# The clamp and the shift of a weight decoder, with their constants in a PSUM column

## Chip, cores, metric

The kernel runs on one core of a Trainium2 chip. The metric is the time of one execution on the device in microseconds (us); lower is better. The engines are TensorE (PE), VectorE (DVE, `V` in the code), ScalarE (ACT, `A`), GpSimd (POOL, `G`) and SyncE (SP, `DQ`), which issues transfers.

## What is computed

```python
X = np.fft.fft(np.fft.fft(x, axis=1), axis=2).real          # x: 2 x 3008 x 256
X = X.reshape(6016, 256)
X = (1 / (1 + np.exp(-(X @ w_gate))) * (X @ w_val)) @ w_out  # layer 1, width 1536
h = X @ w_in                                                 # layer 2, width 2048
out = (h * np.cos(h)) @ w_out2
```

All weights come in as float64, read by the kernel as pairs of 32-bit words, and are turned into float32 on the chip.

## The kernel before

**Work.** The transform has three stages. Stage A (up to about 40 us) multiplies sixteen chunks of x as they arrive. Stages B and C (40 to 83 us) are sixteen blocks of matmuls in a fixed order: twelve of stage B (L399/L400), whose outputs ACT casts to D2h (L419) and DVE subtracts to D2l (L423), and four of stage C (L437), copied out by DVE (L445) or ACT (L448) into `eo`, the activations. Two more blocks of stage C lie inside the first steps of layer 1. Blocks take PSUM banks in turn (`bank()`, `nbank`).

Layer 1 has 72 steps, six token groups by twelve slices of the width. In step s PE does `ab(s, 0)` into banks 4 and 5 and `ab(s, 1)` into banks 6 and 7 (L493 to L495), then the output matmuls of step s−4 (L533, L535, L536), 24 matmuls in all. DVE does `even(s)` (two L511, from banks 4 and 5) and `tokens(s)` (two L519, from banks 6 and 7); ACT the sigmoid (L667) and the high parts (L607, L608); POOL two products (L523) and an accumulating transfer (L546) into gh. `ab(s+1, 0)` waits for `even(s)`, and `ab(s+1, 1)` for `tokens(s)`. Layer 2 follows (L575 and others); it has no decoding.

**Decoding.** The weights are 35 units, all but one of 128 x 512 numbers. A unit's steps (`dec_steps`, `hilo_steps`) are a load by SP (L148), Abs and Copy on ACT (L123, L124), clamp (L127), shift (L129) and OR (L131) on DVE, an integer add on POOL (L134), for the units of the first weights an add and a subtraction of halves (L155, L156), a cast on ACT (L139) and a subtraction on DVE or POOL (L140). Clamp and shift are `tensor_scalar` with two immediate constants, and `every` gives them the tile as two interleaved halves. A unit lives in one of the buffers `eo` until the transform writes there, or in a stage buffer in D.

**What sets the order.** A planner writes each engine's order when the program is built: `clk` holds an estimated time for each engine, `fill` puts a decode step in front of a regular instruction where its estimated cost fits, and `finish` writes out what is left of a unit at once. Two of the four stage buffers, marked `TWO`, lie where `tokens(2)` and later ones write. So from step 2 on:

```python
for un in [un for un in live if un[1] and un[1][1] < (TWO if s < 2 else ALWAYS)]:
    finish(un)
free[:] = [bf for bf in free if bf[1] == ALWAYS or bf[1] == TWO and s == 0]
tokens(s)
```

Of the kernel before, what the change touches and what calls it, by code (L numbers as in the profile page):

```python
# [12 lines left out]
U32 = mybir.dt.uint32  # L13
AF = mybir.ActivationFunctionType
ALU = mybir.AluOpType
# [29 lines left out]
FMIN = float(np.uint32(0x38000000).view(np.float32)) * 2.0 ** -80  # L45
FMAX = float(np.uint32(0x47EFFFFF).view(np.float32)) * 2.0 ** -80
# [3 lines left out]
def fft_moe_moe(ctx: ExitStack, tc: tile.TileContext, x, x0, head, w1, w1s, wo1, w2, t1, t3, out):  # L50
# [10 lines left out]
    V, A, G, PE = nc.vector, nc.scalar, nc.gpsimd, nc.tensor  # L61
# [8 lines left out]
    ps = pp.tile([128, 8, 512], F32, name="ps")  # L70
# [35 lines left out]
    def spend(e, us, after=0.0):  # L106
        clk[e] = max(clk[e], after) + us
        return clk[e]

    def dec_steps(buf, n):  # L110

        r = buf[:, 0:2 * n].rearrange("p (n t) -> p n t", t=2)
        lo, hi = r[:, :, 0], r[:, :, 1]
        t = buf[:, 2 * n:3 * n]
        u = t.bitcast(U32)

        def every(a):

            return a.rearrange("p (n k) -> p k n", k=2)

        return [

            (A, .52, lambda: A.activation(out=t, in_=hi, func=AF.Abs, scale=2.0 ** -80)),  # L123
            (A, .52, lambda: A.activation(out=lo.bitcast(I32), in_=lo.bitcast(U32), func=AF.Copy,  # L124
                                          scale=2.0 ** -29)),

            (V, .34, lambda: V.tensor_scalar(out=every(t), in0=every(t), scalar1=FMIN, scalar2=FMAX,  # L127
                                             op0=ALU.max, op1=ALU.min)),
            (V, .34, lambda: V.tensor_scalar(out=every(u), in0=every(u), scalar1=3, scalar2=0x7FFFFFFF,  # L129
                                             op0=ALU.logical_shift_left, op1=ALU.bitwise_and)),  # L130
            (V, .6, lambda: V.scalar_tensor_tensor(out=u, in0=hi.bitcast(U32), scalar=0x80000000, in1=u,  # L131
                                                   op0=ALU.bitwise_and, op1=ALU.bitwise_or)),

            (G, 1.23, lambda: G.tensor_tensor(out=t.bitcast(I32), in0=t.bitcast(I32), in1=lo.bitcast(I32),  # L134
                                              op=ALU.add)),
        ]
# [64 lines left out]
    def fill(e, until):  # L201

        while True:
            for un in live:
                step = un[2][0]
                if step[0] is VG and e is G and max(un[3], clk[V]) + VADV < max(un[3], clk[G]):
                    continue
                if e in step[0] if step[0] is VG else e is step[0]:
                    if max(un[3], clk[e]) + cost(step, e) <= until:
                        step_of(un, e)  # L210
                        break
            else:
                if e is DQ and len(todo) > held[0] and clk[e] + 1.5 <= until:
                    for bf in free:
                        if bf[2] <= until and max(clk[e], bf[2]) + LIFE <= bf[1]:
                            start(bf)
                            break
                    else:
                        return
                    continue  # L220
                return

    def regular(e, us, at=0.0):

        fill(e, at)
        return spend(e, us, at)
# [50 lines left out]
    def slot(t, us, ahead):  # L277
        while after:
            after.pop(0)()
        for _ in range(2):  # L280
            for e, k in zip((DQ, A, G, V), ahead):
                fill(e, t + us + k)

    with tc.tile_pool(name="xp", bufs=1) as xp:

        raws = [xp.tile([128, 2 * JC, 2, 64], F32, name=f"raw{i}") for i in range(NX2)]
        xs = xp.tile([128, 2, 128], F32, name="xs")
        half = xp.tile([128, B, 2, 24], F32, name="half")  # L290

        def rows(e, out, src):
            for k in range(3):
                e.dma_start(out=out[k:128:4], in_=src[32 * k:32 * (k + 1)])

        def load_x2(p):

            raw, src = raws[p % NX2].rearrange("p (c j) s n -> p c j s n", c=2), x[:, 2 * p:2 * p + 2]
            if p % NX2:
                rows(DQ, raw, src)  # L300
            else:
                DQ.dma_start(out=raw[0:96], in_=src)
            spend(DQ, 2.1)

        warm = xp.tile([128, 128], F32, name="warm")
        DQ.dma_start(out=hd[0:96], in_=head)
        DQ.dma_start(out=raws[0][0:96, JH:JC], in_=x[:, 0, JH:JC])
        DQ.dma_start(out=raws[0][0:96, JC:2 * JC], in_=x[:, 1])
        G.memset(warm, 0.0)
        V.memset(hd[96:128], 0.0)  # L310
        V.memset(hd2, 0.0)
        V.memset(raws[0][96:128], 0.0)
        G.memset(raws[1], 0.0)
        V.memset(raws[2], 0.0)
        V.memset(xs[96:128], 0.0)
        V.memset(halfpi, HALFPI)
        rows(A, hd2, head[:, 0:96])
        A.dma_start(out=xs[0:96], in_=x0)
        clk[DQ] = 1.5
        for p in range(1, NX2):  # L320
            fill(DQ, clk[DQ] + 2.0)
            load_x2(p)


        for _ in range(NWARM):
            PE.matmul(ps[:, 7, 0:128], warm, warm, start=True, stop=True)

        now = 3.5
        clk[V] = clk[G] = clk[A] = 4.5
        for c in range(NJC):  # L330
            if c == 8:
                DQ.dma_start(out=T1, in_=t1)
                DQ.dma_start(out=T3, in_=t3)
                spend(DQ, 1.4)
            slot(now, 1.71, AHA if c < NJC - 2 else (4, .4, 2, .5) if c < NJC - 1 else (4, .1, 2, -.8))
            b0 = 2 * (c % 4)
            for j in range(JC):
                q = ps[:, b0 + j // 4, (j % 4) * 96:(j % 4 + 1) * 96]
                if c == 0 and j < JH:
                    xj = hd[:, 96 + j * 128:96 + (j + 1) * 128]  # L340
                else:
                    xj = raws[c // 2 % NX2][:, c % 2 * JC + j].rearrange("p s n -> p (s n)")
                PE.matmul(q, xj, T2[c // 2 % NX2 > 0], start=True, stop=True)
            if c == CX0:
                for i in range(2):
                    PE.matmul(ps[:, i, 384:480], xs[:, i], T2[0], start=True, stop=True)
            if c % 2 and c // 2 + NX2 < NJC // 2:
                clk[DQ] = max(clk[DQ], now + 1.71)
                load_x2(c // 2 + NX2)

            def evac(c=c, b0=b0, at=now + (1.71 if c else 3.4)):
                src = ps[:, b0:b0 + 2, 0:384].rearrange("p a (q c) -> p c a q", c=96)
                dst = D1[:, :, c * JC:(c + 1) * JC].rearrange("p c (a q) -> p c a q", a=2)
                if c < NJC - 1:
                    regular(A, .7, at)
                    A.copy(dst, src)
                else:
                    regular(V, .5, at - .85)
                    V.tensor_copy(dst[:, :, 0], src[:, :, 0])
                    regular(A, .4, at)  # L360
                    A.copy(dst[:, :, 1], src[:, :, 1])
                if c == CX0:

                    A.mul(half, ps[:, 0, 384:480].rearrange("p (b s k) -> p b s k", b=B, s=2), .5)
                    f128 = ps[:, 1, 384:480].rearrange("p (b s k) -> p b s k", b=B, s=2)
                    d = D1[:, :, 0].rearrange("p (b s k) -> p b s k", b=B, s=2)
                    for r, sg in ((slice(0, 64), .5), (slice(64, 128), -.5)):
                        for cs in range(2):  # L370
                            V.scalar_tensor_tensor(
                                out=d[r, :, cs], in0=f128[r, :, 1 - cs], scalar=(sg if cs else -sg),
                                in1=half[r, :, cs], op0=ALU.mult, op1=ALU.add)
                    spend(A, .2)
                    spend(V, .5, clk[A])

            after.append(evac)
            now += 1.71 if c else 3.4
# [5 lines left out]
    T3h = fp2.tile([128, 5, 128], F32R, name="T3h")  # L384
    T3l = fp2.tile([128, 2, 128], F32R, name="T3l")

    nbank = [0, 8]

    def bank():
        nbank[0] = (nbank[0] + 1) % nbank[1]  # L390
# [431 lines left out]
```

## Time and profile before

| | us |
|---|---|
| three runs, lowest / median / highest | 1037.24 / 1037.32 / 1041.18 |
| profiled execution, first to last instruction (its span) | 1037.8 |
| busy: PE / DVE / ACT / POOL | 1004.8 / 779.9 / 766.1 / 668.7 |
| mean granted clock of TensorE, share of full speed | 0.988 |

The profile gives no time for the profiled execution besides its span, which is 0.5 us above the median. PE is the engine that is nearly always busy; a change can show where PE waits or where its clock is below 1.00.

### The profile page before, as it was taken

Reading aid. Unit: us, or ns where it says so; the run is one execution under the profiler, and the core shown is the slowest. Engines: PE = TensorE matmul, PEld = TensorE weight load, DVE = VectorE, ACT = ScalarE, POOL = GpSimd, SP = SyncE. Lnnn points to the kernel's source line nnn. Section 1 sums busy time; section 2 is a strip of 40 time slices with the busy share of each in tenths; the row PEclk is TensorE's granted clock in tenths of the full one; section 3 lists DMA queues with packets and bytes.
Section 4 is the critical chain, followed back from the end, with each engine's and each line's share of the span. In section 5 each row is a group of like instructions: output and inputs, shape, how many; then the busy total and the mean of one; then the engine's idle time right before and its main releaser. Section 6 shows DMA issues by size and latency. Waiting matters only on the chain.

```text
span 1037.8 us, 13153 instructions
## 1 busy us (share of the span) xinstructions
PE 1004.8 (97%) x4566; PEld 835.8 (81%) x4566; DVE 779.9 (75%) x1029; ACT 766.1 (74%) x1208; POOL 668.7 (64%) x521
## 2 busy tenths in 40 slices
PE   8888899999898999999999999999999999999998
PEld 8877688788786888888788888888888888888886
DVE  5698887877778777776577777777777777777775
ACT  4765466567555667675698888988889888888886
POOL 3686687777666778776364656657466565665753
PEclk9998999999998999999999999999999999999999
DMA  9711457566664666688600000000000000000000
GB/s 293 234 68 53 88 128 173 123 139 136 154 144 106 140 150 150 140 229 218 176 1 20 1 21 0 21 21 1 20 1 21 20 1 21 0 20 21 1 20 21
DMA packets 25363, 85.59 MB, mean 82 GB/s; under 512 B 3248, under 2 KB 6640, under 8 KB 24624
## 3 DMA queue, kind: packets, MB, share of 16 engines
q0 software_dynamic: 10368, 37.02, 19.0%
q1 hardware_dynamic: 14672, 47.59, 13.6%
q8 instruction: 36, 0.59, 0.2%
q14 instruction: 31, 0.25, 0.1%
q10 hardware_dynamic: 256, 0.14, 0.1%
HBM read 33.16 MB, written 14.56 MB: 46 GB/s over the span
## 4 chain that ended last, share of the span: by engine, by line
PE 83%; DVE 9%; DMA 2%; ACT 2%; issue 2%; POOL 1%; SPq 0%; DVEq 0%; ACTq 0%; POOLq 0%
PE ps L575 25%; PE ps L493 14%; PE ps L494 14%; PE ps L495 13%; PE ps L533 5%; PE ps L535 5%; PE ps L536 5%; DVE D L519 4%; DVE D L127 2%; PE ps L437 1%; DMA gh<-D 1%; DVE D L129 1%; DMA eo<-in_w_dram 1%; ACT gh L607 1%; DVE D L511 1%
## 5 line engine op out<-in xcount | busy, mean ns | idle before, releaser
L601 POOL TENSOR_TENSOR h<-D,h 128x502 fp32r<-128x502 f32 x191 | 285.4, 1494 | 214.9 <-ACT h L600 203.1
L575 PE MATMUL ps<-h,wr 128*128 128x502 f32 x1152 | 291.8, 389 | 0.0
L493 PE MATMUL ps<-es,wr 128*128 128x502 f32 x672 | 265.5, 395 | 16.4 <-DVE D L519 10.0
L494 PE MATMUL ps<-es,wr 128*128 128x502 f32 x672 | 264.2, 393 | 0.0
L495 PE MATMUL ps<-es,wr 128*128 128x502 f32 x672 | 263.3, 392 | 0.0
L575 PEld LDWEIGHTS ps<-h,wr 128*128 128x128 f32 x1152 | 217.4, 189 | 44.7
L523 POOL TENSOR_TENSOR D<-D 128x502 f32<-128x502 f32 x144 | 185.1, 1335 | 101.0 <-ACT D L667 99.4
L586 DVE SCALAR_TENSOR_TENSOR D<-D,ps 128x502 f32<-128x502 int32 x192 | 130.2, 678 | 117.9 <-POOL h L601 109.1
L519 DVE TENSOR_TENSOR D<-D,ps 128x1004 f32<-128x1004 f32 x144 | 172.9, 1201 | 54.0 <-PE ps L495 30.3
L667 ACT ACTIVATE D<-D 128x1004 f32<-128x1004 f32 x72 | 75.2, 1044 | 157.3 <-DVE D L519 157.3
L493 PEld LDWEIGHTS ps<-es,wr 128*128 128x128 f32 x672 | 127.4, 190 | 47.7 <-DVE D L519 13.2
L587 DVE SCALAR_TENSOR_TENSOR D<-D 128x502 f32<-128x502 int32 x192 | 144.9, 755 | 6.6
L495 PEld LDWEIGHTS ps<-es,wr 128*128 128x128 f32 x672 | 127.8, 190 | 26.9
L494 PEld LDWEIGHTS ps<-es,wr 128*128 128x128 f32 x672 | 127.9, 190 | 25.5
L585 ACT ACTIVATE D<-ps 128x502 int32<-128x502 f32 x192 | 113.2, 590 | 46.8 <-PE ps L495 44.7
L593 DVE TENSOR_TENSOR D<-D,ps 128x502 f32<-128x502 f32 x192 | 128.9, 671 | 16.1 <-ACT D L592 16.1
L591 ACT ACTIVATE D<-D 128x502 f32<-128x502 f32 x192 | 119.2, 621 | 12.7 <-DVE D L587 10.4
L511 DVE SCALAR_TENSOR_TENSOR D<-eo,w,ps 128x502 f32<-128x502 f32 x144 | 101.8, 736 | 32.2 <-PE ps L495 31.8
L592 ACT ACTIVATE D<-D 128x502 f32<-128x502 f32 x192 | 120.0, 625 | 6.1
L600 ACT CAST h<-D 128x502 fp32r<-128x502 f32 x192 | 114.6, 597 | 0.2 <-DVE D L593 0.2
L535 PE MATMUL ps<-gh,wr 128*128 128x502 f32 x288 | 113.7, 395 | 0.0
L536 PE MATMUL ps<-gh,wr 128*128 128x502 f32 x288 | 112.6, 391 | 0.0
(86 smaller groups left out, 1071.1 us busy)
## 6 DMA issues: line engine op xcount, KB each, us to landing
gh<-D POOLq DMA_DIRECT2D x72, 502.0 KB, 4.8
D<-in_w_dram SPq DMA_DIRECT2D x17, 512.0 KB, 5.1
ws<-D SPq DMA_DIRECT2D x16, 512.0 KB, 3.6
wr<-ws SPq DMA_DIRECT2D x16, 512.0 KB, 4.1
out_dram<-D SPq DMA_DIRECT2D x24, 251.0 KB, 3.4
eo<-in_w_dram SPq DMA_DIRECT2D x11, 512.0 KB, 6.8
raw<-in_x_dram SPq DMA_DIRECT2D x15, 256.0 KB, 5.9
D<-in_wo_dram SPq DMA_DIRECT2D x5, 512.0 KB, 4.5
```

The lines of the kernel that those rows point to most:

```text
L493: PE.matmul(o, w_hi, m_hi, start=first, stop=False)
L494: PE.matmul(o, w_lo, m_hi, start=False, stop=False)
L495: PE.matmul(o, w_hi, m_lo, start=False, stop=last)
L519: V.tensor_tensor(out=gv[s][:, :, c:c + PC], in0=sas, in1=ps[:, 6:8, 0:PC], op=op)
L523: G.tensor_tensor(out=gv[p][:, 1, m], in0=gv[p][:, 1, m], in1=gv[p][:, 0, m], op=ALU.mult)
L535: PE.matmul(o, WO1[:, f, 0, m], h[:, 0, sl], start=(f == 0), stop=False)
L536: PE.matmul(o, WO1[:, f, 1, m], h[:, 0, sl], start=False, stop=False)
L575: PE.matmul(o, WO2[:, f, i, d * 128:(d + 1) * 128], h[:, m], start=(f == 0 and i == m == 0), stop=(f == NF2 - 1 and m == 1))
L586: V.scalar_tensor_tensor(out=r, in0=k, scalar=-C1, in1=h, op0=ALU.mult, op1=ALU.add)
L587: V.scalar_tensor_tensor(out=r, in0=k, scalar=-C2, in1=r, op0=ALU.mult, op1=ALU.add)
L593: V.tensor_tensor(out=r, in0=r, in1=ps[:, 4 + s % 4, 0:PC], op=ALU.mult)
L601: (V if s == N2S - 1 else G).tensor_tensor(out=h[:, 1], in0=r, in1=f32(h[:, 0]), op=ALU.subtract)
```

## The change

Two columns of PSUM bank 7 (510 and 511) are set at the start to the upper limit of the clamp and to the mask of the shift. Clamp and shift become `scalar_tensor_tensor` on DVE: one immediate constant, and the other from that column, broadcast over the tile; the tile is read and written in its plain order. The blocks of stages B and C take banks 0 to 6 in turn, as their outputs would overwrite the columns. In the planner both steps cost 0.6 for 0.34.

```diff
@@ -107,6 +107,16 @@
         clk[e] = max(clk[e], after) + us
         return clk[e]
 
+    cmax, cmask = ps[:, 7, 510:511], ps[:, 7, 511:512].bitcast(U32)
+
+    def clamp(t):
+        V.scalar_tensor_tensor(out=t, in0=t, scalar=FMIN, in1=cmax.to_broadcast(list(t.shape)),
+                               op0=ALU.max, op1=ALU.min)
+
+    def shift(u):
+        V.scalar_tensor_tensor(out=u, in0=u, scalar=3, in1=cmask.to_broadcast(list(u.shape)),
+                               op0=ALU.logical_shift_left, op1=ALU.bitwise_and)
+
     def dec_steps(buf, n):
 
         r = buf[:, 0:2 * n].rearrange("p (n t) -> p n t", t=2)
@@ -114,20 +124,14 @@
         t = buf[:, 2 * n:3 * n]
         u = t.bitcast(U32)
 
-        def every(a):
-
-            return a.rearrange("p (n k) -> p k n", k=2)
-
         return [
 
             (A, .52, lambda: A.activation(out=t, in_=hi, func=AF.Abs, scale=2.0 ** -80)),
             (A, .52, lambda: A.activation(out=lo.bitcast(I32), in_=lo.bitcast(U32), func=AF.Copy,
                                           scale=2.0 ** -29)),
 
-            (V, .34, lambda: V.tensor_scalar(out=every(t), in0=every(t), scalar1=FMIN, scalar2=FMAX,
-                                             op0=ALU.max, op1=ALU.min)),
-            (V, .34, lambda: V.tensor_scalar(out=every(u), in0=every(u), scalar1=3, scalar2=0x7FFFFFFF,
-                                             op0=ALU.logical_shift_left, op1=ALU.bitwise_and)),
+            (V, .6, lambda: clamp(t)),
+            (V, .6, lambda: shift(u)),
             (V, .6, lambda: V.scalar_tensor_tensor(out=u, in0=hi.bitcast(U32), scalar=0x80000000, in1=u,
                                                    op0=ALU.bitwise_and, op1=ALU.bitwise_or)),
 
@@ -308,6 +312,8 @@
         DQ.dma_start(out=raws[0][0:96, JC:2 * JC], in_=x[:, 1])
         G.memset(warm, 0.0)
         V.memset(hd[96:128], 0.0)
+        V.memset(cmax, FMAX)
+        V.memset(cmask, 0x7FFFFFFF)
         V.memset(hd2, 0.0)
         V.memset(raws[0][96:128], 0.0)
         G.memset(raws[1], 0.0)
@@ -384,7 +390,7 @@
     T3h = fp2.tile([128, 5, 128], F32R, name="T3h")
     T3l = fp2.tile([128, 2, 128], F32R, name="T3l")
 
-    nbank = [0, 8]
+    nbank = [0, 7]
 
     def bank():
         nbank[0] = (nbank[0] + 1) % nbank[1]
```

Lines move with the change: clamp L127 is now L113, shift L129 is L117, OR L131 is L135, L134 is L138, L139/L140 are L143/L144, and from L399 on numbers are larger by 6 (L511 is L517, L519 is L525, L423 is L429).

**First place: DVE at step 2 of layer 1.** The pieces begin with the second copy out of stage C's last blocks (`eo_70<-ps`) and show the even part of step 2 and its tokens; `wr` is the tile of decoded weights, and D holds the stage buffers. Before:

```order
L445 COPY eo_70<-ps 128x502 x2
L511 SCALAR_TENSOR_TENSOR D_73<-eo_65,w_71,ps 128x502 x2
L519 TENSOR_TENSOR D_73<-D_73,ps 128x2x502 x2
L511 SCALAR_TENSOR_TENSOR D_73<-eo_65,w_71,ps 128x502 x2
L519 TENSOR_TENSOR D_73<-D_73,ps 128x2x502 x2
```

With the change:

```order
L451 COPY eo_70<-ps 128x502 x2
L517 SCALAR_TENSOR_TENSOR D_73<-eo_65,w_71,ps 128x502 x2
L113 SCALAR_TENSOR_TENSOR D_73<-D_73,ps 128x512
L117 SCALAR_TENSOR_TENSOR D_73<-D_73,ps 128x512
L135 SCALAR_TENSOR_TENSOR D_73<-D_73 128x512
L144 TENSOR_TENSOR wr<-D_73,wr 128x2x256
L113 SCALAR_TENSOR_TENSOR D_73<-D_73,ps 128x512
L117 SCALAR_TENSOR_TENSOR D_73<-D_73,ps 128x512
L135 SCALAR_TENSOR_TENSOR D_73<-D_73 128x512
L144 TENSOR_TENSOR wr<-D_73,wr 128x2x256
L525 TENSOR_TENSOR D_73<-D_73,ps 128x2x502 x2
```

Two units, of which no DVE step has been done by then, are now finished between the even part and the tokens of step 2; before, nothing stood there.

**Second place: DVE in the steps of layer 1 in which the first unit is decoded after that.** Each pair L511, L519 is a step. Before:

```order
L127 TENSOR_SCALAR D_73<-D_73 128x2x256
L129 TENSOR_SCALAR D_73<-D_73 128x2x256
L511 SCALAR_TENSOR_TENSOR D_73<-eo_65,w_71,ps 128x502 x2
L519 TENSOR_TENSOR D_73<-D_73,ps 128x2x502 x2
L131 SCALAR_TENSOR_TENSOR D_73<-D_73 128x512
L511 SCALAR_TENSOR_TENSOR D_73<-eo_65,w_71,ps 128x502 x2
L519 TENSOR_TENSOR D_73<-D_73,ps 128x2x502 x2
```

With the change:

```order
L113 SCALAR_TENSOR_TENSOR D_73<-D_73,ps 128x512
L517 SCALAR_TENSOR_TENSOR D_73<-eo_65,w_71,ps 128x502 x2
L525 TENSOR_TENSOR D_73<-D_73,ps 128x2x502 x2
L117 SCALAR_TENSOR_TENSOR D_73<-D_73,ps 128x512
L517 SCALAR_TENSOR_TENSOR D_73<-eo_65,w_71,ps 128x502 x2
L525 TENSOR_TENSOR D_73<-D_73,ps 128x2x502 x2
L135 SCALAR_TENSOR_TENSOR D_73<-D_73 128x512
L517 SCALAR_TENSOR_TENSOR D_73<-eo_65,w_71,ps 128x502 x2
L525 TENSOR_TENSOR D_73<-D_73,ps 128x2x502 x2
```

Clamp and shift stood in one gap and the OR in the next; now each of the three has a gap of its own.

**Third place: DVE at the end of the transform,** up to the even part of step 0; `eo_69` in the rows of before is a unit that was put into a buffer of the activations. Before:

```order
L129 TENSOR_SCALAR D_73<-D_73 128x2x256
L131 SCALAR_TENSOR_TENSOR D_73<-D_73 128x512
L423 TENSOR_TENSOR D2l<-ps,D2h 128x256 x2
L127 TENSOR_SCALAR eo_69<-eo_69 128x2x256
L129 TENSOR_SCALAR eo_69<-eo_69 128x2x256
L131 SCALAR_TENSOR_TENSOR eo_69<-eo_69 128x512
L423 TENSOR_TENSOR D2l<-ps,D2h 128x256 x2
L511 SCALAR_TENSOR_TENSOR D_73<-eo_65,w_71,ps 128x502 x2
```

With the change:

```order
L117 SCALAR_TENSOR_TENSOR D_73<-D_73,ps 128x512
L429 TENSOR_TENSOR D2l<-ps,D2h 128x256 x2
L135 SCALAR_TENSOR_TENSOR D_73<-D_73 128x512
L113 SCALAR_TENSOR_TENSOR D_73<-D_73,ps 128x512
L117 SCALAR_TENSOR_TENSOR D_73<-D_73,ps 128x512
L135 SCALAR_TENSOR_TENSOR D_73<-D_73 128x512
L429 TENSOR_TENSOR D2l<-ps,D2h 128x256 x2
L517 SCALAR_TENSOR_TENSOR D_73<-eo_65,w_71,ps 128x502 x2
```

The decoding of that unit is gone from here, and what stands ahead of the last D2l is another unit's clamp, shift and OR.

## Rows read from the trace of the kernel before

**Rows 1.** The page, first part: busy time of each engine.

```profile
PE 1004.8 (97%) x4566; PEld 835.8 (81%) x4566; DVE 779.9 (75%) x1029; ACT 766.1 (74%) x1208; POOL 668.7 (64%) x521
```

**Rows 2.** Busy us (x instructions) by engine, in three stretches.

```profile
core 0: us, PE busy (x) PEld busy (x) DVE busy (x) ACT busy (x) POOL busy (x), PEclk, DMA share, GB/s
40.40:83.20 42.80, 36.38 (x241) 32.98 (x241) 42.51 (x66) 28.58 (x66) 33.62 (x28) 0.92 0.29 101
...
103.60:340.00 236.40, 222.99 (x943) 181.43 (x943) 189.43 (x195) 142.40 (x166) 172.99 (x152) 0.97 0.61 133
340.00:496.00 156.00, 156.00 (x686) 129.22 (x685) 117.96 (x133) 98.98 (x113) 117.09 (x104) 1.00 0.72 171
```

**Rows 3.** PE's waits: us in total, times, longest us.

```profile
PE ps L493 <- DVE D L519: 10.0, 7, 1.7
PE ps L493 <- DVE D L511: 6.4, 4, 3.0
PE ps L437 <- DVE D2l L423: 4.5, 2, 2.5
PE ps L437 <- ACT D2h L419: 1.8, 1, 1.8
PE ps L533 <- DMA gh<-D: 1.1, 1, 1.1
```

**Rows 4.** Clamp and shift by line: ns min/median/max, first and last start.

```profile
L127 DVE TENSOR_SCALAR D<-D x22: 418/620/6433, 67.6 to 448.4; 128x512 f32<-128x512 f32 x22
L129 DVE TENSOR_SCALAR D<-D x22: 428/430/5380, 68.6 to 448.8; 128x512 uint32<-128x512 uint32 x22
```

**Rows 5.** DVE's timeline: start us, us.

```profile
111.40 6.43 DVE L127 TENSOR_SCALAR D<-D 128x512 f32<-128x512 f32 x1
```

**Rows 6.** POOL's timeline over the same time.

```profile
111.59 1.55 POOL L140 TENSOR_TENSOR es<-eo,es 128x502 fp32r<-128x502 f32 x1
112.81 2.78 POOL L523 TENSOR_TENSOR D<-D 128x502 f32<-128x502 f32 x2
115.26 1.17 POOL L546 DMA_DIRECT2D gh<-D  x1
115.86 1.68 POOL L140 TENSOR_TENSOR es<-eo,es 128x502 fp32r<-128x502 f32 x1
```

**Rows 7.** PE's timeline just behind it, with its waits in brackets.

```profile
119.00 0.50 PE L493 MATMUL ps<-es,wr 128*128 128x502 f32 x1 [1.86 <-DVE D L511]
122.31 0.69 PE L493 MATMUL ps<-es,wr 128*128 128x502 f32 x1 [1.68 <-DVE D L519]
```

**Rows 8.** Other lines on DVE: ns min/median/max.

```profile
L511 DVE SCALAR_TENSOR_TENSOR D<-eo,w,ps x144: 719/737/742, 86.1 to 493.8; 128x502 f32<-128x502 f32 x144
L586 DVE SCALAR_TENSOR_TENSOR D<-D,ps x192: 677/678/681, 500.0 to 1026.1; 128x502 f32<-128x502 int32 x192
L131 DVE SCALAR_TENSOR_TENSOR D<-D x22: 682/684/1652, 70.4 to 453.8; 128x512 uint32<-128x512 uint32 x22
```

**Rows 9.** Busy us of L127, then of L129, on DVE.

```profile
40.40:83.20 42.80, 8.40 (x10) 0.92 0.29 101
40.40:83.20 42.80, 8.99 (x9) 0.92 0.29 101
```

**Rows 10.** PE's timeline in the transform: a wait for D2l.

```profile
77.28 0.50 PE L437 MATMUL ps<-D2l,T3h 128*128 128x502 f32 x1 [2.47 <-DVE D2l L423]
```

**Rows 11.** DVE's timeline at step 2 of layer 1.

```profile
97.86 1.38 DVE L511 SCALAR_TENSOR_TENSOR D<-eo,w,ps 128x502 f32<-128x502 f32 x2
99.34 1.20 DVE L519 TENSOR_TENSOR D<-D,ps 128x1004 f32<-128x1004 f32 x1
```

**Rows 12.** PE's timeline behind it.

```profile
101.91 0.75 PE L493 MATMUL ps<-es,wr 128*128 128x502 f32 x1 [1.64 <-DVE D L519]
```

**Rows 13.** Later steps of a unit: ns min/median/max.

```profile
L134 POOL TENSOR_TENSOR D<-D x22: 1293/1592/1928, 71.9 to 460.8; 128x512 int32<-128x512 int32 x22
L139 ACT CAST wr<-D x6: 601/618/622, 75.2 to 141.9; 128x512 fp32r<-128x512 f32 x6
L140 DVE TENSOR_TENSOR wr<-eo,wr x3: 674/692/693, 16.5 to 67.0; 128x512 fp32r<-128x512 f32 x3
```

## Prediction

> **What bounds the kernel now.** I read the page's first part, then the busy time by stage, the waits of TensorE, and the decode steps line by line. TensorE (PE) is busy 97% of the 1037.8 us span [rows 1], so time can only be won where it waits or runs at a low clock. [rows 2] says where that is. From 340 us on it is full at clock 1.00. In the transform's later stages (40.4 to 83.2) it is busy 36.38 of 42.80 us at clock 0.92, so 6.4 us idle and about 0.08 × 42.8 = 3.4 us of clock: 9.8 us in all. In layer 1 up to 340 us it is busy 222.99 of 236.40 at 0.97: 13.4 us idle and some 7 us of clock. VectorE (DVE) is what it waits for [rows 3]: 10.0 us for the token sums and 6.4 us for the even parts of layer 1, and 4.5 us for the low parts D2l of the transform, plus 1.8 us for ACT's D2h.
>
> DVE has time on average; what makes it late is the clamp (L127) and the shift (L129). On the 22 units in D they take a median of 620 and 430 ns, but up to 6433 and 5380 ns [rows 4]. The long ones stand where GpSimd (POOL) runs without a gap: the clamp of 111.40 ends at 117.83, and POOL works from 111.59 to 117.54 [rows 5, 6]. PE then waits 1.86 us for the even part and 1.68 us for the tokens [rows 7]. DVE instructions with one SBUF input and one PSUM input do not do that: L511 stays between 719 and 742 ns over 144 executions and L586 between 677 and 681 over 192, both beside a busy POOL [rows 8].
>
> The Trainium skill has the mechanism (SBUF — State Buffer, section Who interferes with whom): a DVE instruction in a two-port mode takes a port pair that it shares with GpSimd, the other blocks fully, and one with at most one SBUF input outside these modes does not contend. The trace agrees on the last point with 677 to 681 ns. The page has the lock held for one instruction; by that the loser would wait one POOL instruction, at most 1.7 us in [rows 6], and a clamp would last about 2.1 us. The row shows 6.43, held over five POOL rows, and the measured one counts.
>
> **The change, part by part.** *The operation.* No row shows a PSUM column broadcast along a tile. The nearest rows are L586 (678 ns, same form, immediate scalar, 502 columns) and L511 (737) [rows 8]. I take 0.70 us. From below: nothing under 0.43 (the unhindered clamp and shift, minima of [rows 4]); from above, L511's 0.74. So each op is dearer than an unhindered one by 0.27 us and cheaper than the held ones.
>
> *Layer 1.* Before, clamp and shift stand together in a gap between the tokens of one step and the even part of the next, and the OR (L131) in the following one. After, each has a gap of its own (order, second place). From 340 on PE does 686 matmuls in 156 us [rows 2], 0.2274 us each, so a step of 24 takes 5.46 us and there are 28.6 of them. DVE is busy 117.96 us in these, 4.1 per step with its decoding; so about 1.3 us of a step is free and 0.70 fits. The 36 clamps and shifts that stay in these gaps therefore cost PE nothing. What comes back is the idle time behind the held ones: 13.4 us less the 1.1 us for a gh transfer [rows 3] is 12.3, and 6 to 7 us of low clock that follow those waits: 18.5 us. The OR still has two SBUF inputs and can be stretched to 1.65 us [rows 8]; that I charge with 1 us. **Gain 17.5 us**, bounds 12 (no clock comes back) and 20.4 (all idle and clock).
>
> *The transform.* DVE is busy 42.51 of 42.80 us [rows 2]: saturated. 10 clamps and 9 shifts take 8.40 + 8.99 = 17.4 us of that [rows 9], 0.92 each. The changed order has 17 there at 0.70, 11.9 us: 5.5 us less. With the planner's cost 0.6 for 0.34, two units of the output weights are no longer decoded here, and three L155/L156 halves and a subtraction go to POOL: some 3 us more. DVE falls from 42.5 to about 34 us, and the two waits for D2l, 4.5 us together [rows 3], the longer 2.47 [rows 10], are much shorter than the 8 us that it is ahead by then. I leave 1 us of wait in front of the first column matrix (its D2l stands behind a shift and two subtractions) and 1 us of clock. **Gain 8 us**, bounds 4 and 9.8. Seven banks cost nothing that I see: each bank is emptied more than two blocks before it comes round again.
>
> *Step 2 of layer 1.* This is the price. The two units that were not decoded sit in stage buffers whose place the token sums of step 2 overwrite, so the program finishes them there, on the spot (order, first place): clamp, shift, OR, then POOL's add, ACT's cast, DVE's subtraction, and the same for the second unit, all ahead of the tokens of step 2. ACT is in order, and the second unit's Abs stands behind the first one's cast, so nothing of the second chain overlaps. Before, the tokens began at 99.34, right after the even part of 97.86, and PE went on at 101.91 [rows 11, 12]. Now one chain is 3 × 0.70 + 1.30 (L134 at its shortest) + 0.62 (L139) + 0.69 (L140) [rows 13] = 4.71 us, two are 9.4, with handovers 9.8. PE has only the even matmuls of step 3 to do meanwhile, then stands. Queued behind the tokens on DVE is the even part of step 3, on ACT the sigmoid, on POOL the products of step 2; all move by the same amount. **Loss 10 us**, bounds 8.5 and 13 (L134's longest 1.93 twice, and a few more slow matmuls after the longer stop).
>
> *The rest.* The two memsets at the start and the waits on bank 7 in the first stage (clamps wait for matmuls and copies of the fourth bank pair) come where PE waits for the input; I charge 0.5 us, between 0 and 2. Layer 2 has no decoding and moves as a whole; the stores and reloads of its weights come a few places later on SP and are needed only from 496 us on.
>
> **Sum.** 1037.8 − 17.5 − 8 + 10 + 0.5 = 1022.8 for the profiled execution. The median of the runs is 1037.32, 0.5 below that span, so the forecast is **1022 us**.
>
> The Trainium skill has a rule that speaks against the change (PSUM — Partial Sum Buffer, section on bank collisions): two engines must never be in one bank at the same time, reads included, so software has to order them, and no run here shows what happens otherwise. By the rule each clamp has to lie between the matmuls of two steps on bank 7, where the tokens lie already; what it costs if there is no room is rival (a).
>
> **Rivals.** (a) *Every gap becomes a wait: slower.* Reading one PSUM word 512 times, or the ordering on bank 7, makes the op long. Up to 1.3 us it is free in layer 1; beyond, 36 gaps lose the excess, and the transform's gain is gone at 17.4 / 17 = 1.0 us. With 10.5 us fixed price and 17.5 us from layer 1, it turns to a loss when the op is over 1.3 + 7/36 = 1.5 us; at 2 us the time is 1037.8 − 7 + 36 × 0.7 = 1056. For it speaks only that no row has the form; against it, L586 and L511. Chance 5%. (b) *The transform stays as it was* because ACT and POOL, not DVE, hold the chain: POOL is busy 33.6 of 42.8 us there [rows 2] and gets the moved halves; and step 2 costs 13: 1037.8 − 17.5 − 1 + 13 = 1032. Chance 12%. (c) *The new op is held by POOL as well*, so the change does not do what it says: layer 1 gives nothing back, step 2 still costs 10, the transform gains 3 from the lighter load: 1045; if held half as much, 1036. Chance 9%. (d) *Step 2 is cheap*: part of its 10 us is absorbed, since the DVE-bound waits of the next steps vanish and the transform ends earlier than needed: with 6 us lost, 20 and 9.8 gained, 1014. Chance 12%.
>
> **How the numbers follow.** The sum's own case has 62%; with its bounds it runs from 1037.3 − 20.4 − 9.8 + 8.5 = 1016 to about 1031 (layer 1 at 12, the transform at 8, step 2 at 13). A difference under 0.5% (5 us) can hardly be told from none here. Faster by more than that: the sum, (d), and most of (b): 0.84. Within: the rest of (b), the half-held case of (c): 0.08. Slower: (a) and the other part of (c): 0.08. For 8 in 10 the range reaches from (d)'s 1014 to just past (b)'s 1032: 1014 to 1033.
>
> **What the changed profile would show.** Right: the two new lines between 0.67 and 0.76 us with hardly any spread; no wait of PE for the even part between 110 and 340; PE's stretch from 40 to the start of layer 1 some 8 us shorter; one PE wait of about 10 us for the tokens near 93, with L113, L117, L135 and L144 in pairs on DVE ahead of it. Wrong: new lines over 1 us or stretched beside POOL; the waits for D2l still there; a wait of several us for weights that arrive late in step 2; new PE waits in each step behind a clamp.

## The result and the profile after

Four runs of the change took 1027.11 to 1031.73 us, median 1028.8; four of before had a median of 1039.25. The ratio is 0.9909 with a 95% interval of 0.9882 to 0.9935: about 10 us faster. The forecast was 1022 us with a range of 1014 to 1033. The profiled execution took 1028.23 us at a span of 1026.3.

The page of the changed kernel, answering [rows 1]:

```profile
PE 996.3 (97%) x4566; PEld 831.8 (81%) x4566; DVE 770.0 (75%) x1031; ACT 765.4 (75%) x1207; POOL 667.7 (65%) x522
```

PE lost 8.5 us of busy time that was only slower matmuls, and 3 us of idle time, in a span shorter by 11.5. The new lines, and the OR, with ns min/median/max (answers to [rows 4, 8]):

```profile
L113 DVE SCALAR_TENSOR_TENSOR D<-D,ps x23: 670/680/689, 68.0 to 434.8; 128x512 f32<-128x512 f32 x23
L117 DVE SCALAR_TENSOR_TENSOR D<-D,ps x23: 671/680/689, 69.7 to 440.2; 128x512 uint32<-128x512 uint32 x23
L135 DVE SCALAR_TENSOR_TENSOR D<-D x23: 682/686/5417, 70.4 to 445.7; 128x512 uint32<-128x512 uint32 x23
```

Clamp and shift now always take 0.67 to 0.69 us. It is the OR that now reaches 5.4 us. PE's waits after the change, in total, times and longest (answers to [rows 3]):

```profile
PE ps L499 <- DVE D L525: 16.7, 5, 11.7
PE ps L349 <- DMA raw<-in_x_dram: 3.5, 2, 1.9
PE ps L332 <- DVE ps L316: 1.7, 1, 1.7
...
PE ps L499 <- DVE D L517: 0.6, 2, 0.4
PE ps L443 <- DVE D2l L429: 0.5, 1, 0.5
PE ps L349 <- DVE eo L117: 0.3, 1, 0.3
```

The wait for D2l went from 4.5 to 0.5 us, the one for the even part from 6.4 to 0.6; the one for the tokens grew from 10.0 to 16.7 us, with a single wait of 11.7 in it. The wait of L332 is that of the first matmuls for the memset of a column in bank 7. The time by stretch, answering [rows 2]:

```profile
core 0: us, PE busy (x) PEld busy (x) DVE busy (x) ACT busy (x) POOL busy (x), PEclk, DMA share, GB/s
...
21.00:30.00 9.00, 8.78 (x50) 8.81 (x51) 4.92 (x11) 4.09 (x7) 5.67 (x5) 0.62 0.57 193
...
43.30:76.90 33.60, 32.93 (x241) 30.52 (x241) 30.42 (x59) 25.13 (x61) 27.56 (x25) 1.00 0.24 80
76.90:107.00 30.10, 17.09 (x71) 13.24 (x71) 22.76 (x31) 14.65 (x22) 17.65 (x16) 0.82 0.23 70
107.00:330.00 223.00, 220.39 (x960) 181.53 (x959) 180.98 (x199) 144.11 (x167) 174.71 (x154) 0.99 0.62 138
330.00:485.00 155.00, 153.33 (x673) 126.50 (x672) 122.69 (x130) 97.52 (x111) 116.82 (x103) 1.00 0.74 175
```

The transform (43.3 to 76.9) is at full clock with 0.7 us idle, and DVE, forecast to fall from 42.5 to about 34 us there, is busy 30.42. The 30 us behind it hold only 17.09 us of matmuls at clock 0.82. And from 21 to 30 us, in the first stage, the mean granted clock was 0.62, where before had 1.00: 50 matmuls in 8.78 busy us, and 77 in 8.62 before.

To see where the time moved, I cut each profiled execution at the same four events: the first matmul of stage B, the first of layer 1, the end of the tokens of step 2, and the start of the last L511 (now L517) of layer 1. In the change these lie at 43.4, 76.9, 105.6 and 482.3 us, and the end at 1026.3. The stages in us, from the timelines; they are differences of rounded times, so a cell can be off by 0.1:

| kernel | first stage | transform | steps 0 to 2 | rest of layer 1 | after it | span |
|---|---|---|---|---|---|---|
| before | 40.5 | 42.6 | 18.8 | 391.9 | 544.0 | 1037.8 |
| the change | 43.4 | 33.5 | 28.7 | 376.7 | 544.0 | 1026.3 |
| e1_cost_only | 41.4 | 36.0 | 28.3 | 396.6 | 544.0 | 1046.3 |
| e2_op_only | 44.2 | 39.8 | 18.7 | 373.6 | 543.9 | 1020.2 |
| e3_sbuf_const | 40.9 | 42.1 | 29.3 | 390.5 | 544.9 | 1047.7 |
| e4_op_late | 38.9 | 38.7 | 19.5 | 373.2 | 544.2 | 1014.5 |
| e5_no_finish | 39.7 | 36.8 | 18.8 | 389.5 | 544.6 | 1029.4 |
| e6_finish | 39.5 | 36.0 | 33.7 | 374.7 | 544.1 | 1028.0 |
| e7_clamp_twice | 43.2 | 37.8 | 29.7 | 380.0 | 544.1 | 1034.7 |
| e8_seven_banks | 41.0 | 41.1 | 19.4 | 389.0 | 544.3 | 1034.8 |
| e9_skip_two | 41.1 | 39.6 | 18.8 | 370.8 | 545.6 | 1015.9 |
| e10_old_op_skip | 42.6 | 42.6 | 18.7 | 372.1 | 544.0 | 1020.0 |
| e11_combined | 41.0 | 37.9 | 18.6 | 373.8 | 544.3 | 1015.6 |

A row is one execution. How far a stage wanders by itself is seen in e8 and e10: e8 has the order of before in layer 1 and is 2.9 us shorter there; e10 has the first stage of before, instruction for instruction, and is 2.1 us longer there.

### The profile page after: what moved, and what is told of

Its sections match the earlier page's. It is cut to its first block, busy times and chain, and to the rows that moved or that the text cites. A ratio compares the mean times of both kernels' runs of the same rounds, so it can differ in the third digit from the quotient of the medians.

```text
span 1026.3 us, 13186 instructions
## 1 busy us (share of the span) xinstructions
PE 996.3 (97%) x4566; PEld 831.8 (81%) x4566; DVE 770.0 (75%) x1031; ACT 765.4 (75%) x1207; POOL 667.7 (65%) x522
## 4 chain that ended last, share of the span: by engine, by line
PE 87%; DVE 4%; DMA 3%; ACT 2%; issue 2%; POOL 1%; ACTq 0%; SPq 0%; DVEq 0%; POOLq 0%
PE ps L581 25%; PE ps L499 14%; PE ps L500 14%; PE ps L501 14%; PE ps L539 5%; PE ps L541 5%; PE ps L542 5%; DVE D L525 3%; PE ps L349 2%; DMA gh<-D 1%; DMA raw<-in_x_dram 1%; PE ps L443 1%; ACT gh L613 1%; DMA xs<-in_x_dram 1%; PE ps L405 0%
## 5 line engine op out<-in xcount | busy, mean ns | idle before, releaser
L499 PE MATMUL ps<-es,wr 128*128 128x502 f32 x672 | 263.8, 393 | 17.3 <-DVE D L525 16.7
L525 DVE TENSOR_TENSOR D<-D,ps 128x1004 f32<-128x1004 f32 x144 | 172.9, 1201 | 52.7 <-PE ps L501 32.9
L499 PEld LDWEIGHTS ps<-es,wr 128*128 128x128 f32 x672 | 127.0, 189 | 46.6 <-DVE D L525 18.8
L517 DVE SCALAR_TENSOR_TENSOR D<-eo,w,ps 128x502 f32<-128x502 f32 x144 | 102.0, 736 | 23.4 <-PE ps L501 22.9
```

Source lines behind the costliest of these rows:

```text
L499: PE.matmul(o, w_hi, m_hi, start=first, stop=False)
L525: V.tensor_tensor(out=gv[s][:, :, c:c + PC], in0=sas, in1=ps[:, 6:8, 0:PC], op=op)
```

## The experiments

The theory was that an input in PSUM frees clamp and shift from GpSimd, that this gives time back in the transform and in layer 1, and that the planner's higher cost takes 10 us in step 2. The first rival: the new order gives the time back and not the instruction.

**e1_cost_only and e2_op_only: order and instruction apart.** e1 is the kernel before with the new costs (the first line of clamp and of shift):

```diff
-            (V, .34, lambda: V.tensor_scalar(out=every(t), in0=every(t), scalar1=FMIN, scalar2=FMAX,
+            (V, .6, lambda: V.tensor_scalar(out=every(t), in0=every(t), scalar1=FMIN, scalar2=FMAX,
...
-            (V, .34, lambda: V.tensor_scalar(out=every(u), in0=every(u), scalar1=3, scalar2=0x7FFFFFFF,
+            (V, .6, lambda: V.tensor_scalar(out=every(u), in0=every(u), scalar1=3, scalar2=0x7FFFFFFF,
```

e2 is the change with the old costs:

```diff
-            (V, .6, lambda: clamp(t)),
-            (V, .6, lambda: shift(u)),
+            (V, .34, lambda: clamp(t)),
+            (V, .34, lambda: shift(u)),
```

> The kernel before, with the planner's cost of clamp and shift raised from 0.34 to 0.6 and nothing else: the old instructions in nearly the new order, with two units finished at once in step 2. If the operation is what gave time back (my theory), the long clamps and shifts stay, layer 1 has its waits of 10 us and more after step 3, and step 2 costs about 10 us: 1038 to 1050 us. If the new order gave it back (rival), PE has few waits after step 3 and the time is about that of the change, 1026 to 1030 us.

> The change with the planner's cost put back to 0.34: the new instructions and seven banks, and in step 2 of layer 1 nothing is finished ahead of the tokens. My theory: no wait of 11.7 us in step 2, the clamps stay at 0.68 us, and of the 11.5 us gained the 10 of step 2 come on top, less what the fuller transform takes: 1015 to 1020 us. Rival (the order did it): 1030 to 1040 us.

e1: 1042.95 us, ratio 1.0049 (1.0027 to 1.0072), slower than before. e2: 1023.24 us, ratio 0.9856 (0.9833 to 0.9879), faster than the change, but 3 us above the range of my theory. So the instruction gives the time, and the order as a whole takes some back. PE's waits in e1:

```profile
PE ps L493 <- DVE D L519: 20.6, 7, 11.2
PE ps L493 <- DVE D L511: 6.2, 5, 2.0
```

With the old instructions both waits of layer 1 are there, and the long one of step 2 (11.2 us) beside them. In the table, steps 0 to 2 last 28 to 29 us in both kernels with cost 0.6 and 18.7 to 18.8 in both with 0.34: the 10 us are the order's alone. The transform is otherwise than I had it: with the old instruction the order alone takes 42.6 to 36.0, with the old order the instruction alone 42.6 to 39.8. (e2 also has seven banks; e8, seven banks with the old instruction, has 41.1, so as little as 1.3 us of that may be the instruction's.) e2's first stage, PE's timeline:

```profile
15.57 2.92 PE L349 MATMUL ps<-hd,raw 128*128 128x96 f32 x24 [1.28 <-DVE eo L117]
...
26.26 17.10 PE L349 MATMUL ps<-hd,raw 128*128 128x96 f32 x136 [2.63 <-DVE eo L117]
```

PE stands 1.28 and 2.63 us for a shift (L117): the program has its next matmuls, which write bank 7, wait until the shift has read it.

**e3_sbuf_const: the input in PSUM, or the form of the instruction.** The two constants become columns of an SBUF tile:

```diff
-    halfpi = cpool.tile([128, 1], F32, name="halfpi")
+    halfpi3 = cpool.tile([128, 3], F32, name="halfpi")
+    halfpi = halfpi3[:, 0:1]
...
-    cmax, cmask = ps[:, 7, 510:511], ps[:, 7, 511:512].bitcast(U32)
+    cmax, cmask = halfpi3[:, 1:2], halfpi3[:, 2:3].bitcast(U32)
```

> The change with the two constants in SBUF instead of PSUM: same instructions, same order, both tensor inputs in SBUF. If an input in PSUM is what frees the operation from GpSimd, clamp and shift are stretched again to several us where GpSimd runs without a gap, and PE waits for DVE in layer 1: 1035 to 1050 us. If the form of the instruction or the plain access pattern is enough, they stay at 0.7 us and the time is 1026 to 1030 us; stage A then also starts without waits on bank 7.

It took 1048.93 us, ratio 1.0098 (1.0075 to 1.0121). Clamp and shift by line, ns min/median/max:

```profile
L114 DVE SCALAR_TENSOR_TENSOR D<-D,halfpi x23: 684/1010/6683, 69.5 to 457.4; 128x512 f32<-128x512 f32 x23
L118 DVE SCALAR_TENSOR_TENSOR D<-D,halfpi x23: 675/908/1631, 71.9 to 462.8; 128x512 uint32<-128x512 uint32 x23
```

The same instructions in the same order, and the clamp is held for 6.68 us again; the median rises from 0.68 to 1.01. It is the input in PSUM. The Trainium skill says as much (SBUF — State Buffer, section Who interferes with whom): a DVE instruction with two SBUF inputs contends with a GpSimd instruction that reads SBUF; one with at most one, outside the two-port modes, does not. The runs agree for the new form, with 684 to 6683 ns against 670 to 689.

**e4_op_late: the first stage without bank 7.** e2 with the old instructions until stage A is planned:

```diff
     def clamp(t):
+        if early[0]:
+            V.tensor_scalar(out=every(t), in0=every(t), scalar1=FMIN, scalar2=FMAX,
+                            op0=ALU.max, op1=ALU.min)
+            return
...
     now += 1.2
+    early[0] = False
...
-            PE.matmul(ps[:, 7, 0:128], warm, warm, start=True, stop=True)
+            PE.matmul(ps[:, 6, 0:128], warm, warm, start=True, stop=True)
```

The shift is changed likewise.

> As e2_op_only, but in the first stage, up to 40 us, clamp and shift are the old instructions, and the warm matmuls use bank 6: DVE has no wait on bank 7 there. If the 2.9 us that the first stage lost come from bank 7, the first block of stage B starts at about 40.5 us again and the time is 2 to 4 us below e2_op_only. If they come from the transfers of x or a low clock by chance, it starts as late as there.

1018.23 us, ratio 0.9801 (0.9778 to 0.9824) against e2's 0.9856; the intervals do not meet. That is 5 us below e2, more than the 2 to 4 expected. The first stage takes 38.9 us against 44.2 (38.9 to 41.1 in e4, e5, e6, e9 and e11, whose first stage is alike). The three kernels that read bank 7 there (the change, e2 and e7) need 43.2 to 44.2 us for the first stage, the ten others 38.9 to 42.6.

**e5_no_finish and e6_finish: the light transform without step 2's price.** Both are e4 with cost 0.6 behind the first stage. The rule that e5 adds opens no `TWO` buffer for a new unit once the engine's estimated time is past 50 us, so that `finish` finds nothing at step 2. In e6 LAST lies so far out that the rule never holds.

```diff
-            (V, .34, lambda: clamp(t)),
-            (V, .34, lambda: shift(u)),
+            (V, .34 if early[0] else 0.6, lambda: clamp(t)),
+            (V, .34 if early[0] else 0.6, lambda: shift(u)),
...
-                        if bf[2] <= until and max(clk[e], bf[2]) + LIFE <= bf[1]:
+                        if bf[2] <= until and max(clk[e], bf[2]) + LIFE <= bf[1] and not (bf[1] == TWO and clk[e] > LAST):
...
+    LAST = 50
```

> The old instructions in the first stage as in e4_op_late, the new ones at cost 0.6 afterwards, and a rule in the planner that starts no unit in the two overwritten stage buffers once its load queue stands past 50 us: nothing is finished at once in step 2, and the transform keeps the light load of the change. If the 10 us of step 2 and the 2.9 us of the first stage are all that the change gives away, the time is 1028.8 - 10 - 3 to - 5, that is 1013 to 1017 us, at or up to 4 us below e4_op_late. If the lighter transform is worth nothing, or the units left for later cost as much elsewhere, it is above e4_op_late, 1018 to 1026 us.

> e5_no_finish without its rule: in step 2 an OR and a subtraction of one unit and a shift, OR and subtraction of another stand ahead of the tokens. My theory: this costs two chains of add, cast and subtraction on top of three DVE steps, 3 x 0.7 + 2 x 2.7 = 7.5 us, and PE shows one wait of 8 to 10 us before the tokens of step 2: 6 to 8 us above e5_no_finish. If the finish mostly overlaps with what PE has to do, the two are within 2 us.

e5 took 1030.94 us (0.9916, 0.9896 to 0.9936), above what either theory gave it; e6 1031.9 (0.9935, 0.9915 to 0.9954), 1 us above e5, with overlapping intervals, and not the expected 6 to 8, as e5 lost in layer 1 what it had won. Step 2 did what was meant: 18.8 us in e5, 33.7 in e6, where PE waits:

```profile
PE ps L515 <- DVE D L541: 15.4, 4, 11.5
...
PE ps L459 <- DVE eo L467: 3.4, 1, 3.4
```

The first row holds e6's finish, one wait of 11.5 us, more than the 8 to 10 expected; the second is a copy out of PSUM that came late on DVE. But e5's rest of layer 1 is 389.5 us, 15 longer than e6's. Two things stand there. PE waits for weights that were left too late:

```profile
156.49 0.50 PE L557 MATMUL ps<-gh,wr 128*128 128x502 f32 x1 [0.66 <-ACT wr L157]
158.80 0.75 PE L558 MATMUL ps<-gh,wr 128*128 128x502 f32 x1 [1.82 <-POOL wr L158]
```

And the OR is held, on DVE, up to 7 us (ns min/median/max):

```profile
L149 DVE SCALAR_TENSOR_TENSOR D<-D x22: 679/684/6980, 67.5 to 448.2; 128x512 uint32<-128x512 uint32 x22
```

Four of its executions took 1.7, 4.9, 7.0 and 7.0 us, two of e6's 1.7 and 5.4. Whether an OR is held depends on where the planner puts it. I had no theory for that. So I listed for all kernels so far the gaps of layer 1 in which a decode instruction of DVE took over 4 us. Counted by the step whose even part follows, modulo 12, they are the gaps 5 to 7, in every kernel, with the old instruction and with the OR. In this part of each twelve steps GpSimd has two subtractions `es<-eo` for the next token group beside its products and transfers. The row of the change on DVE, and POOL over it:

```profile
246.34 5.42 DVE L135 SCALAR_TENSOR_TENSOR D<-D 128x512 uint32<-128x512 uint32 x1
```

```profile
246.17 0.88 POOL L552 DMA_DIRECT2D gh<-D  x1 [1.59 <-issue]
246.78 1.60 POOL L144 TENSOR_TENSOR es<-eo,es 128x502 fp32r<-128x502 f32 x1
248.02 2.83 POOL L529 TENSOR_TENSOR D<-D 128x502 f32<-128x502 f32 x2
250.46 1.23 POOL L552 DMA_DIRECT2D gh<-D  x1
251.06 1.74 POOL L144 TENSOR_TENSOR es<-eo,es 128x502 fp32r<-128x502 f32 x1
```

The OR begins 0.17 us after the first of these rows and ends at 251.76, inside the last of them (251.06 to 252.80). In between POOL has no pause.

**e9_skip_two and e10_old_op_skip: those gaps left empty.** On e4, and on the kernel before:

```diff
+    SKIP = (5, 6)
...
-            ahead(V, now + 3 * MM)
+            if s % NF1 not in SKIP:
+                ahead(V, now + 3 * MM)
             even(s)
```

In e10 SKIP is (5, 6, 7). `ahead` is what puts decode steps of DVE into the gap in front of an even part.

> e4_op_late with one more rule: no decode step stands on DVE ahead of the even parts of steps 5 and 6 of each twelve, the two gaps in which GpSimd has two subtractions of activations beside its usual work. My theory is that the OR, with two inputs in SBUF, is held only there: no execution of it over 1.7 us, no wait of PE behind it near 310 us, and 1 to 3 us below e4_op_late. If holds come from any busy GpSimd, they appear in other gaps and the time is that of e4_op_late or above.

> The kernel before, old instructions and all banks, with no decode step ahead of the even parts of steps 5, 6 and 7 of each twelve. If the holds belong to these gaps, the old clamp and shift stay under 2 us in layer 1 as well, PE loses its waits after 110 us, and most of the 18 us of layer 1 come back without the new operation: 1019 to 1026 us, with the transform as before. If the old form is held wherever GpSimd works, long clamps appear in other gaps and the time stays at 1033 to 1040 us.

e9: 1017.57 us, ratio 0.979 (0.9774 to 0.9806). Its OR, ns min/median/max:

```profile
L149 DVE SCALAR_TENSOR_TENSOR D<-D x22: 683/686/1661, 69.2 to 430.3; 128x512 uint32<-128x512 uint32 x22
```

e10: 1020.36 us, ratio 0.9809 (0.9781 to 0.9836). Its clamp and shift, which are the old instructions:

```profile
L127 DVE TENSOR_SCALAR D<-D x22: 415/710/1504, 69.7 to 431.0; 128x512 f32<-128x512 f32 x22
L129 DVE TENSOR_SCALAR D<-D x22: 428/429/1074, 70.7 to 431.9; 128x512 uint32<-128x512 uint32 x22
```

None is held for more than 1.7 us in either, e10's OR with its longest of 1.66 us included. The rest of layer 1 takes 370.8 and 372.1 us, against 391.9 before and 376.7 with the change. e9 is 0.7 us below e4, though, and the intervals overlap: that it is faster than e4 is not shown. e10 is the stronger result: three gaps left empty in the kernel before give twice what the change gives, without a new instruction.

**e7_clamp_twice: a longer operation.**

```diff
-            (V, .6, lambda: clamp(t)),
+            (V, .6, lambda: [clamp(t), clamp(t)]),
```

> The change with each clamp executed twice, which changes no value, in the same order otherwise. It tests what a longer operation costs. By the free 1.3 us in each step of layer 1, a second 0.68 us beside the first costs nothing there; the transform has ten more such rows while DVE has some 3 us to spare, and step 2 gets 1.4 us longer: 1029 to 1035 us. If every gap is tight, 20 gaps lose up to 0.7 us each on top: 1040 to 1047 us.

1035.29 us, ratio 0.9965 (0.9948 to 0.9982), 6.5 us above the change and just past the range given. The 46 clamps on D (23 twice) keep their length:

```profile
L113 DVE SCALAR_TENSOR_TENSOR D<-D,ps x46: 673/686/690, 69.4 to 443.9; 128x512 f32<-128x512 f32 x46
```

Of the profiled 8.4 us, the transform has 4.3, step 2 1.0 and the rest of layer 1 3.3, against the 2.9 by which that stage differs between before and e8. So a step of layer 1 does hold twice 0.68 us, as worked out, or nearly: if every one of 20 gaps had lost 0.7 us, it would be 14.

**e8_seven_banks: seven banks alone.** `nbank = [0, 8]` becomes `[0, 7]` in the kernel before.

> The kernel before with banks 0 to 6 in turn in the transform and nothing else. If seven banks are enough, the time is that of before, 1036 to 1040 us. If a block then waits for a bank, PE shows waits for the copies out of PSUM between 40 and 83 us and the time is 2 us or more above.

1038.59 us, ratio 1.0005 (0.999 to 1.002): nothing, as charged.

**e11_combined: a middle cost on top.** e9 with cost 0.45 behind the first stage and the rule of e5:

```diff
+            (V, .34 if early[0] else 0.45, lambda: clamp(t)),
+            (V, .34 if early[0] else 0.45, lambda: shift(u)),
...
+    LAST = 50
```

> e9_skip_two with a cost of 0.45 after the first stage and the rule of e5_no_finish for the two overwritten buffers, so that some decode steps move out of the transform and nothing is finished at once in step 2. If the waits for D2l of e9_skip_two (4.8 us) shrink with the load on DVE and layer 1 keeps its free gaps, the transform is 1 to 3 us shorter and the time 1014 to 1017 us. If the moved steps cost as much in layer 1, the time is that of e9_skip_two, 1017 to 1019 us.

1018.23 us, ratio 0.9796 (0.9776 to 0.9816). The transform is 1.7 us shorter than e9's and layer 1 3.0 longer: no gain over e9.

## Why the prediction was right, and where it was off

**The operation** was right: 0.68 us for the forecast 0.70, without spread, and the input in PSUM is the reason (e3).

**Step 2** was right, in place and price. From the start of layer 1 to the end of the tokens of step 2 the change takes 28.7 us, before 18.8: 9.9 for the forecast 10. PE's wait grew by as much, from 1.64 us to 11.67. The rows on DVE, answering [rows 11]:

```profile
91.57 1.38 DVE L517 SCALAR_TENSOR_TENSOR D<-eo,w,ps 128x502 f32<-128x502 f32 x2
92.86 0.69 DVE L113 SCALAR_TENSOR_TENSOR D<-D,ps 128x512 f32<-128x512 f32 x1
93.58 0.69 DVE L117 SCALAR_TENSOR_TENSOR D<-D,ps 128x512 uint32<-128x512 uint32 x1
94.31 0.69 DVE L135 SCALAR_TENSOR_TENSOR D<-D 128x512 uint32<-128x512 uint32 x1
97.50 0.69 DVE L144 TENSOR_TENSOR wr<-D,wr 128x512 fp32r<-128x512 f32 x1 [2.50 <-ACT wr L143]
...
99.55 0.69 DVE L135 SCALAR_TENSOR_TENSOR D<-D 128x512 uint32<-128x512 uint32 x1
102.43 0.69 DVE L144 TENSOR_TENSOR wr<-D,wr 128x512 fp32r<-128x512 f32 x1 [2.19 <-ACT wr L143]
103.15 2.44 DVE L525 TENSOR_TENSOR D<-D,ps 128x1004 f32<-128x1004 f32 x2
```

Between even part and tokens stand two chains; the idle times are the two trips over POOL and ACT. Their rows for the first unit:

```profile
95.24 1.58 POOL L138 TENSOR_TENSOR D<-D 128x512 int32<-128x512 int32 x1
```

```profile
96.85 0.62 ACT L143 CAST wr<-D 128x512 fp32r<-128x512 f32 x1 [2.96 <-POOL D L138]
```

PE meanwhile, answering [rows 12] in its first row:

```profile
105.64 0.79 PE L499 MATMUL ps<-es,wr 128*128 128x502 f32 x1 [11.67 <-DVE D L525]
...
255.77 0.49 PE L499 MATMUL ps<-es,wr 128*128 128x502 f32 x1 [1.69 <-DVE D L525]
```

From 92.86 to 103.12 us the two chains take 10.3, where I had worked out 9.8: the add took 1.58 us for the first unit and 1.27 for the second, where I had put in its shortest, 1.30, for both, and the handovers came to 0.7 for my 0.4.

**The transform** came out at 9.1 us for 8, but the two halves of the working were the wrong way round, so that the sum fits is in part luck. I gave 5.5 us to the shorter instructions and 3 to what moves out. e1 and e2 show 6.6 us for the order alone and 2.8 for the instruction alone, and 9.1 for both at once. The instruction does shorten DVE's work, but most of what PE waited for goes when fewer decode steps stand ahead of the D2l that it needs: DVE's busy time there falls to 33.9 us in e1 and only to 38.3 in e2.

**Layer 1** is the term that was mis-sized: 15.2 us for 17.5 (391.9 to 376.7). The step that failed is that clamp, shift and OR each in a gap of its own cost nothing but 1 us for a stretched OR. The instruction alone gives 18.3 us (before to e2), as much as the rows promised; the order takes 3.1 of it back (e2 to the change) and, with the old instruction, 4.7 (before to e1, whose profiled execution is 5.2 us above its median, so that this may be too much). [rows 8] had shown the OR at 1.65 us, and I took its longest of that order for its longest of any; in the change two ORs are held in layer 1, for 5.42 and 4.88 us. In the second row above PE waits 1.69 us at 255.77, behind the OR of 246.34 and what follows it, and 0.40 us for the even part at 252.46, where I had forecast no such wait. With two SBUF inputs the OR belongs to the held kind, as the Trainium skill has it (SBUF — State Buffer, section Who interferes with whom). It is not that more ORs stand in the gaps 5 to 7: the change has six there and before has five, none of which takes over 0.69 us. What differs in gap 5 is when the OR starts. This is one of before, with the transfer on POOL beside it:

```profile
182.62 0.68 DVE L131 SCALAR_TENSOR_TENSOR D<-D 128x512 uint32<-128x512 uint32 x1
```

```profile
182.59 0.87 POOL L546 DMA_DIRECT2D gh<-D  x1 [1.60 <-issue]
```

It starts 0.03 us behind the transfer and is not held, although a subtraction and two products follow on POOL without a pause; the two of the change that are held start 0.17 and 0.12 us behind it. Of the 21 ORs that stand in gap 5 in the kernels up to e8, the ten that start 0.00 to 0.12 us behind the transfer take 0.68 or 0.69 us, and the eleven that start 0.12 to 0.18 us behind it take 4.9 to 7.0. So about a tenth of a microsecond seems to decide; no experiment moved the start alone.

The differences of 3 to 5 us that the order makes to layer 1 are about as large as the 2.9 us between before and e8; the held ORs with PE's waits behind them are seen, their exact price is not.

**The first stage** was charged 0.5 us, with 2 as the upper end, and took 2.9. The waits on bank 7 are real (0.3 us in the change, 3.9 in e2), and e4 wins e2's stage back. In the change itself the first stage also has the stretch at a mean clock of 0.62 from 21 to 30 us, behind a wait of 1.87 us for x. That bank 7 leads to it is only argued: e10, whose first stage is that of before, shows 0.69 from 10 to 21 us and is 2.1 us longer there than before, so a low stretch comes by itself as well.

**The sum** on the profiled spans was −15 and came to −11.5: 2.3 from layer 1, 2.4 from the first stage, less 1.1 from the transform. That is 3.5 of the 6.8 us between 1022 and 1028.8. 0.3 is rounding, and 3.0 are the step from the span to the runs: I put the median 0.5 us below the profiled span, and it lies 2.5 above. In the change and every experiment the profiled execution takes 1.8 to 2.0 us more than its span, as here 1028.23 against 1026.3. By that the profiled execution of before took some 1039.7, near the later median of before, 1039.25, and not 1037.32.

Of the rivals, (a) and (c) are out by the new lines, 0.67 to 0.69 us each, and e7 shows how much longer they could be; (b) by the transform's 33.5 us; (d) did not come, as step 2 had its full price. That the changed order and not the instruction gives the gain is out by e1 for the whole, though not for the transform.

## What to carry to other kernels

Before changing an instruction that is sometimes long, list where in the loop its long executions stand: here all over 4 us in layer 1 stood in three of twelve gaps, and leaving those empty (e10) was worth 20 us against the change's 10. A planner's cost is a change of order: price the order and the instruction apart, with one kernel for each. And a constant parked in a PSUM bank ties its readers to everybody else who uses that bank.

## What the runs showed that I had not expected

An instruction of DVE with two SBUF inputs is held just as long by GpSimd as the old form: 6.98 us for the OR in e5, over six instructions of POOL in a row, not one. Every long hold had a chain on POOL without a pause beside it, and the same OR beside single POOL instructions stays between 0.68 and 1.7 us (e9). The chain alone is not enough, as the OR of before at 182.62 shows.

A long stop of PE cost hardly more clock than a short one. Behind the 11.67 us stop the next matmuls start 0.42 us apart from 105.64 to 109.57, nine of them, at a granted clock of 0.50, the lower of its two levels (1.2 of 2.4 GHz), and from 111 on it is 1.00. Behind the 1.64 us stop of before eight did so, from 101.91 to 105.38, at 0.51 over that stretch, and from 105.4 on it was 1.00. So the price of step 2 is the two chains and next to nothing else.
